# Half-precision pairs in the gating products, and a block of three experts in four column groups, in a kernel of mLSTM, spatial gating and sticky experts

## The chip, the cores and the metric

The kernel runs on one core of one Trainium2 chip. A core has a matrix engine (TensorE, in the profile PE; its weight loads are listed apart as PEld), three engines that work element by element (VectorE or DVE, ScalarE or ACT, GpSimdE or POOL), and SyncE (SP), which here only starts transfers between the chip's main memory and the core's memories. A matrix product on TensorE takes two operands: one of up to 128 columns is loaded into the array and stays ("weights"), the other streams through it column by column; the sums are written to PSUM, from which DVE or ACT must take them. The metric is the device time of one execution in microseconds (us); less is better.

## What is computed

Three layers follow one another, for 2 batches of 768 tokens (320 features in 8 heads of 40):

```python
# 1. mLSTM: a running matrix memory with gates (here worked out in chunks of 128 tokens)
C = f_stab * C + i_stab * outer(v, k); n = f_stab * n + i_stab * k
y = sigmoid(o_gate) * (C @ q) / max(|n . q|, 1)
# 2. gating products
h = relu(x @ w_in)                        # 320 -> 1024; u, v = the two halves
v_n = (v - mean) / sqrt(var + 1e-6)
v_s = w_spatial @ v_n + b_spatial         # mixes tokens
x2 = (u * v_s) @ w_out                    # 512 -> 320
# 3. eight experts; a token keeps the expert before it while sigmoid(x2 @ w_local) >= 0.5
e = argmax(x2 @ w_gate) or the token's predecessor's e
out = softmax(x2 @ w_gate)[e] * (relu(x2 @ w1[e]) @ w2[e])   # 320 -> 1024 -> 320
```

## The kernel before

**Exact products.** The choice of an expert hangs on small differences, so products are made of pairs: an operand is split into a high part and the remainder (low), and high x high, low x high and high x low are added up in PSUM. In layer 3 and in the token mixing the parts are F16 (`split`, `ws_piece`). In the gating products (x @ w_in and x2, with the tiles `wi`, `xh`, `xl`, `wo_h`, `wo_l`, `gt`) they are F32R, a rounded F32 format of four bytes that TensorE takes in one pass.

**Work of layers 1 and 2.** A chunk of 128 tokens is a number `i` from 0 to 11; `hf` from 0 to 3 is a group of three chunks, `dc` a block of 128 features. `do_ph(i)` makes the v half of x @ w_in, 8 matmuls of 512 columns for each of 12 chunks; `u_steps(hf, dc)` makes the u half, 8 matmuls of 384 columns for each of 16 pairs; `mix_steps` mixes tokens (18 F16 matmuls of 384 columns and one F32R) and multiplies by u; `x2_mm` makes x2, 12 matmuls for each of 12 chunks, of 330 columns in the first nine (10 for the expert choice) and 320 in the last three; `logits` makes the choice for the last three apart, 12 matmuls of 384 columns. `do_xh`/`do_xl`, `conv_in`, `conv_out`, `route_weights` and the end of `mix_steps` make the pairs, the high part on ACT and the remainder on DVE (some on POOL).

**Layer 3.** Tokens are sorted by expert into blocks of 128 rows: four early blocks (100 to 103) from batch 0 alone, five (0 to 4) of one expert each, three spare ones (6 to 8), and block 5, which three rarer experts share: `TILES = ((0, 32, 5), (32, 64, 6), (64, 128, 7))` gives rows 0 to 31 to expert 5, 32 to 63 to expert 6 and 64 to 127 to expert 7. A block is gathered (`gather`, POOL), turned (`turn_rows`), sent through w1 (`up_steps`: PSUM `phT`, then `hh` on ACT and `hl` on DVE, in two halves) and through w2 (`down`: 24 products, one for each of 8 row slices `fc` and 3 pairs, summed in PSUM `py`; then `yt` on ACT and a scatter on POOL). The weights come by SP into four staging tiles `stg` (`ld`) and are split on ACT and DVE (`sp`: `w2h`, then `w2l`). In block 5 each of the 24 products of `down` is three matmuls, one for each expert, whose loaded operand has 32, 32 and 64 columns; they write rows 0, 32 and 64 of `py`. Its result `yl` goes out last, behind a branch for further blocks (`last_blocks`) that this input doesn't take.

**What sets the order.** A table `ORDER` of 1,600 tokens (`bd.5` is the next piece of `down` for block 5) is written out by hand; each engine and each queue runs its own share strictly in that order, and waits on semaphores for the others.

Of the kernel before, what the change touches and what calls it, by code (L numbers as in the profile page):

```python
# [8 lines left out]
F32 = mybir.dt.float32  # L9
F32R = mybir.dt.float32r  # L10
# [33 lines left out]
S_K = 2.0 ** 4  # L44
X_TOP = 5
# [42 lines left out]
Lq.0 R.0 g.0 g.0 g.0 g.0 Lg.0 g.1 g.2 g.0 g.0 g.1 Lt.0 g.0 g.1 s0.0 Lv.0 g.0 g.0 g.1 C.0 s1.0 da.0 C.0 g.1 C.0 g.0 R.17  # L88
Lv.1 de.0 da.0 de.0 g.1 ds.0 C.0 R.1 co.0 g.1 Lq.1 ot.0 C.0 g.1 g.2 C.0 w0.0 g.2 Lt.1 C.1 w1.0 g.2 g.2 C.1 s2.0 w2.0
Lt.2 R.7 g.2 Lg.1 y0.0 g.1 k2.0 y1.0 y2.0 g.1 g.1 g.2 C.1 Lg.2 C.1 Lq.2 g.1 da.1 C.0 C.7 C.1 g.2 s2.1 g.2 g.2 da.1 U.0  # L90
ot.1 de.1 g.2 s0.1 de.1 R.2 g.2 da.2 dn.0 t1.0 xm.0 xc.0 px.0 um.0 Le.1 ds.1 co.1 Lv.2 g.2 w2.1 k2.1 de.2 da.3 C.0 C.1
Le.2 qg.1 da.2 s1.1 C.7 xh.0 U.1 C.2 w0.1 um.1 R.8 s0.2 de.2 xl.0 y0.1 ds.2 Lq.3 ot.2 C.2 co.2 C.1 C.2 Le.3 y2.1 w1.1
C.2 C.2 um.1 C.8 y1.1 C.1 s1.2 Lt.3 w1.2 ph.0 t1.1 Lg.3 ph.0 R.3 w0.2 de.3 k2.2 dn.1 C.8 s2.2 da.3 xm.1 qg.2 um.2 da.4
Lv.3 U.2 y0.2 C.2 C.2 xc.1 um.2 C.2 de.3 s0.3 w2.2 C.3 C.3 y1.2 y2.2 ph.0 s1.3 ds.3 Lg.4 co.3 C.3 qg.3 um.3 w0.3 t1.2
de.4 s2.3 C.3 C.3 px.1 C.3 dn.2 xh.1 da.4 y0.3 R.4 C.4 w2.3 rl.0 w1.3 xm.2 da.5 de.4 y2.3 Le.4 y1.3 xl.1 C.4 xc.2 da.5
Lg.5 ph.1 C.4 k2.3 C.4 U.3 dn.3 C.3 Lq.4 Lt.4 ds.4 co.4 R.5 C.4 bn.0 ot.3 s0.4 Lv.4 C.4 C.3 de.5 s2.4 t1.3 px.2 pw.0
Lq.5 xm.3 ph.1 w0.4 de.5 C.5 s1.4 um.3 Lt.5 w1.4 xh.2 qg.4 ds.5 ph.1 y0.4 xl.2 C.5 ph.2 Le.5 C.5 ot.4 w2.4 C.4 nw.0 ph.2
R.13 C.5 s1.5 C.4 xc.3 Lq.6 nw.0 k2.4 nh.0 y1.4 C.5 y2.4 s0.5 ph.2 C.5 rl.1 um.4 nl.0 Lv.5 w1.5 C.13 Lg.6 R.12 s2.5 C.5
dn.4 C.13 ds.6 qg.5 t1.4 U.4 Lv.6 rl.2 w2.5 um.4 R.14 u.0.0 w0.5 px.3 C.13 u.0.1 xh.3 C.5 de.6 bn.1 y0.5 ot.6 xm.4 C.13
# [62 lines left out]
def mlstm_sgu_sticky_moe(ctx: ExitStack, tc, qk, qk3, vko, ig, fg, w_in, w_out, w_sp, b_sp, w_gate, w_local, w1, w2, out):  # L162
# [132 lines left out]
    def f64_words(raw, n, out=None):  # L295
# [1254 lines left out]
```

## Time and profile before

| | |
|---|---|
| Median of 3 runs | 326.38 us (324.33 to 327.87) |
| Profiled execution, own time | 330.37 us |
| Its span, first to last instruction | 328.6 us |
| PE busy | 304.6 us (93%), 2685 matmuls |
| DVE busy | 263.1 us (80%) |
| ACT busy | 204.2 us (62%) |
| POOL busy | 108.8 us (33%) |
| DMA | 58.22 MB, 177 GB/s over the span |
| Mean granted TensorE clock | 0.996 of full |

The profiled execution is 3.99 us longer than the median of the runs. A matmul's end is modelled in the trace and reaches past the start of the next one, so "PE busy" says that something was under way, and what a matmul costs in a stream is read from the distance between starts.

### The profile page before, as it was taken

The page shows a single profiled execution, that of the slowest core. Times are in us where ns is not written, and L with a number is a line of the kernel's source. Part 1 is how long each engine was busy: PE and PEld are TensorE (multiplying, and loading weights), DVE is VectorE, ACT ScalarE, POOL GpSimd, SP SyncE. Part 2 cuts the span into 40 slices and gives each one's busy share as a digit, 9 for nine tenths or more (in the row PEclk, how much of TensorE's full clock was granted, in tenths as well). Part 3 has the DMA queues.
Part 4 walks back from the last instruction along what each step waited for, and adds up shares of the span by engine and source line. Part 5 has one row for each costly group of instructions (what it writes and reads, how often), then busy time and mean ns, then how long its engine had stood idle before and what let it go on. Part 6 is the DMA issues. An engine that isn't in the chain of part 4 may idle for free. (4 is left out here: it accounts for less than half of the span.)

```text
span 328.6 us, 7571 instructions
## 1 busy us (share of the span) xinstructions
PE 304.6 (93%) x2685; PEld 243.3 (74%) x2685; DVE 263.1 (80%) x655; ACT 204.2 (62%) x455; POOL 108.8 (33%) x150
## 2 busy tenths in 40 slices
PE   2499998999999999989999999999989999999991
PEld 1387895877885797669887677698968889888740
DVE  8999499998878988668776998799986957897810
ACT  1568387678697667683667665857466437666700
POOL 7585156342343202015421223600070605400401
PEclk9999999999999999999999999999999999999998
DMA  6857578665786474900016787796976765957500
GB/s 175 268 138 204 169 215 214 183 217 160 200 274 165 110 178 95 221 30 2 1 51 195 247 224 191 217 311 176 243 211 245 204 228 130 359 185 208 198 21 24
DMA packets 27707, 58.22 MB, mean 177 GB/s; under 512 B 5146, under 2 KB 15676, under 8 KB 27664
## 3 DMA queue, kind: packets, MB, share of 16 engines
q1 hardware_dynamic: 24258, 51.18, 53.7%
q0 software_dynamic: 1456, 4.53, 4.4%
q10 hardware_dynamic: 1950, 1.97, 2.3%
q8 instruction: 23, 0.38, 0.5%
q14 instruction: 20, 0.16, 0.2%
HBM read 53.25 MB, written 4.59 MB: 176 GB/s over the span
## 5 line engine op out<-in xcount | busy, mean ns | idle before, releaser
L1335 PE MATMUL phT<-xgT,w1all 128*128 128x128 f16 (+2 forms) x768 | 41.8, 210 | 0.0
L1335 PEld LDWEIGHTS <-w1all 128*128 128x128 f16 x768 | 39.1, 97 | 1.6
L577 PE MATMUL psS<-qbd,qk 120*128 120x384 f32 (+1 forms) x60 | 27.9, 561 | 10.4 <-DVE m L254 6.1
L790 PE MATMUL pv<-ws_h,vnh 128*128 128x384 f16 x96 | 31.3, 328 | 0.0
L790 PE MATMUL pv<-ws_h,vnl 128*128 128x384 f16 x96 | 31.3, 326 | 0.0
L790 PE MATMUL pv<-ws_l,vnh 128*128 128x384 f16 x96 | 31.3, 326 | 0.0
L1245 DVE SCALAR_TENSOR_TENSOR w2l<-stg,w2h 128x640 f16<-128x640 f32 x36 | 28.7, 819 | 3.1 <-ACT w2h L1243 3.0
L1356 PEld LDWEIGHTS <-hh 128*128 128x128 f16 (+2 forms) x240 | 22.0, 98 | 10.7
L1243 ACT ACTIVATE w1all<-stg 128x1024 f16<-128x1024 f32 (+1 forms) x24 | 22.2, 946 | 10.3 <-DMA stg<-in_moe_w_dram 3.9
L790 PEld LDWEIGHTS <-vnh 128*128 128x128 f16 x192 | 18.6, 97 | 13.5 <-issue 0.8
L1305 POOL DMA_INDIRECT xg<-rows_d,gidx x9 | 10.8, 1203 | 51.3 <-DVE w1all L1262 25.8
L1243 ACT ACTIVATE w2h<-stg 128x640 f16<-128x640 f32 x36 | 25.2, 730 | 3.2 <-DMA stg<-in_moe_w_dram 3.0
L492 POOL TENSOR_SCALAR_AFFINE_SELECT gbc<-gbc 128x512 f32<-128x512 f32 (+1 forms) x18 | 17.4, 967 | 28.8 <-DVE lg L843 10.8
L1245 DVE SCALAR_TENSOR_TENSOR w1all<-stg,w1all 128x1024 f16<-128x1024 f32 (+1 forms) x24 | 26.4, 1103 | 0.5 <-ACT w1all L1243 0.5
L837 PE MATMUL po<-wo_h,gt 128*128 128x330 f32 (+1 forms) x96 | 24.4, 328 | 1.2 <-DVE ut L796 1.2
L1356 PE MATMUL py<-w2h,hl 128*128 128x320 f16 (+2 forms) x88 | 23.7, 303 | 0.0
L1356 PE MATMUL py<-w2h,hh 128*128 128x320 f16 (+2 forms) x88 | 23.7, 303 | 0.0
L1356 PE MATMUL py<-w2l,hh 128*128 128x320 f16 (+2 forms) x88 | 23.7, 303 | 0.0
L1340 ACT ACTIVATE hh<-phT 128x512 f16<-128x512 f32 x26 | 15.3, 592 | 12.5 <-PE phT L1335 12.3
L724 PE MATMUL ph<-wi,xh 128*128 128x512 f32 x60 | 22.8, 457 | 0.0
L1342 DVE SCALAR_TENSOR_TENSOR hl<-phT,hh 128x512 f16<-128x512 f32 x26 | 17.8, 686 | 6.0 <-ACT hh L1340 5.7
L584 DVE TENSOR_TENSOR gbc<-psS,gbc 128x384 f32<-128x384 f32 (+1 forms) x36 | 17.6, 501 | 5.3 <-PE psS L577 5.1
(320 smaller groups left out, 833.8 us busy)
## 6 DMA issues: line engine op xcount, KB each, us to landing
stg<-in_moe_w_dram SPq DMA_DIRECT2D x22, 640.0 KB
stg<-in_moe_w_dram SPq DMA_DIRECT2D x16, 512.0 KB
vko<-in_vko_dram SPq DMA_DIRECT2D x12, 504.5 KB
gbc<-scg SPq DMA_DIRECT2D x6, 512.0 KB
qk<-in_qk_dram SPq DMA_DIRECT2D x8, 360.0 KB
ws<-in_moe_w_spatial_dram SPq DMA_DIRECT2D x6, 384.0 KB
raw<-in_moe_w_in_dram SPq DMA_DIRECT2D x4, 512.0 KB
stg<-in_moe_w_dram SPq DMA_DIRECT2D x8, 256.0 KB
```

The source lines that it names most:

```text
L492: nc.gpsimd.affine_select(out=dm, in_=dm, pattern=[[0, n], [1, P]], compare_op=ALU.is_ge, fill=fill, base=0, channel_multiplier=-1)
L577: nc.tensor.matmul(ps[:, :n * P].rearrange("p (a s) -> p a s", a=n), u["kT"][:, g, :], u["qbd"][:, g:g + 3 * n - 2:3], start=True, stop=True)
L584: nc.vector.tensor_tensor(w, u["ps", g][:, :n * P].rearrange("p (a s) -> p a s", a=n), w, ALU.mult)
L724: nc.tensor.matmul(u["ph"], x_[:, sl], wi[:, wk, DH:], start=(n == 0), stop=(n == len(terms) - 1))
L790: nc.tensor.matmul(pv, x_[i][:, ds_], w_[:, c, ts_], start=False, stop=(n == 18))
L837: nc.tensor.matmul(pos[i], gx[hf, dc][:, sl], wx[:, dc, :cols], start=(n == 0), stop=(n == 11))
L1243: nc.scalar.activation(hi, src, AF.Copy, scale=scale)
L1245: nc.vector.scalar_tensor_tensor(lo, src, scale, hi, ALU.mult, ALU.subtract)
L1335: nc.tensor.matmul(ph[:, f * P + t0:f * P + t1], w_[fc // 2][:, wk, (fc % 2) * P:(fc % 2 + 1) * P], xT[:, xk, t0:t1], start=(n == 0), stop ...
L1340: nc.scalar.activation(hh[:, hs], pf, AF.Relu)
L1342: nc.vector.scalar_tensor_tensor(hl[:, hs], pf, 0.0, hh[:, hs], ALU.max, ALU.subtract)
L1356: nc.tensor.matmul(py[t0:t1], h_[:, fc, t0:t1], ws[w_][:, fc], start=(n == 0), stop=(n == 23))
```

## The change

Layer 2 gets four new scales, powers of two, so that scaling rounds nothing. The tiles `wi`, `wo_h`, `wo_l`, `xh`, `xl` and `gt` become F16. Copies on ACT become copies with a scale, subtractions on DVE become scale-and-subtract, and where sums leave PSUM the scale is taken out again in an instruction that was there before. In `down`, block 5's expert 7 gets two matmuls of 32 loaded columns in place of one of 64. `ORDER` is a new table of the same 1,600 tokens. The copy of the index column `sidx` in the branch stands in both kernels.

```diff
+S_X = 2.0 ** 9
+S_WI = 2.0 ** 6
+S_G = 2.0 ** 10
+S_WO = 2.0 ** 6
 ORDER = '''
-Lq.0 R.0 g.0 g.0 g.0 g.0 Lg.0 g.1 g.2 g.0 g.0 g.1 Lt.0 g.0 g.1 s0.0 Lv.0 g.0 g.0 g.1 C.0 s1.0 da.0 C.0 g.1 C.0 g.0 R.17
+Lg.0 Lv.0 g.0 g.0 g.1 Lq.0 Lt.0 R.0 Lg.1 R.1 g.0 g.0 g.0 s0.0 ot.0 g.0 s2.0 g.0 g.1 g.0 g.2 g.1 g.1 C.0 C.0 g.1 C.0 g.0
...
-    wi = l2.tile([P, 5, DF], F32R, name="wi")
-    wo_h = lk.tile([P, 4, 330], F32R, name="wo_h")
-    wo_l = lk.tile([P, 4, 330], F32R, name="wo_l")
+    wi = l2.tile([P, 5, DF], F16, name="wi")
+    wo_h = lk.tile([P, 4, 330], F16, name="wo_h")
+    wo_l = lk.tile([P, 4, 330], F16, name="wo_l")
...
-            nc.scalar.copy(wi[:, kc, cs], t)
+            nc.scalar.activation(wi[:, kc, cs], t, AF.Copy, scale=S_WI)
             yield
-            nc.vector.tensor_tensor(wi[:, 2 + kc, cs], t, wi[:, kc, cs].bitcast(F32), ALU.subtract)
+            nc.vector.scalar_tensor_tensor(wi[:, 2 + kc, cs], t, S_WI, wi[:, kc, cs], ALU.mult, ALU.subtract)
...
-            xh[hf] = l2.tile([P, 3, HALF], F32R, tag="xh", name="xh", bufs=2)
-            xl[hf] = l2.tile([P, 3, HALF], F32R, tag="xl", name="xl", bufs=2)
+            xh[hf] = l2.tile([P, 3, HALF], F16, tag="xh", name="xh", bufs=2)
+            xl[hf] = l2.tile([P, 3, HALF], F16, tag="xl", name="xl", bufs=2)
...
-        nc.vector.tensor_tensor(xl[hf][:, :, sl], st[i]["px"].rearrange("p (k s) -> p k s", k=3),
-                                xh[hf][:, :, sl].bitcast(F32), ALU.subtract)
+        nc.vector.scalar_tensor_tensor(xl[hf][:, :, sl], st[i]["px"].rearrange("p (k s) -> p k s", k=3), S_X,
+                                       xh[hf][:, :, sl], ALU.mult, ALU.subtract)
...
-        gt = lk.tile([P, 2, HALF], F32R, tag="g", name="gt", bufs=8)
+        gt = lk.tile([P, 2, HALF], F16, tag="g", name="gt", bufs=8)
...
-            parts = [(t0, t1, w2t[e]) for t0, t1, e in TILES]
+            parts = [(t, t + 32, w2t[e]) for t0, t1, e in TILES for t in range(t0, t1, 32)]
```

The first place at which instructions move is TensorE in `down` of block 5, the last work of TensorE (`py_5253` before and `py_5250` after; the third number is how many columns of the operand are loaded, then how many stream). Before:

```order
L1356 LDWEIGHTS hh_4977
L1356 MATMUL py_5253<-w2h_2972,hh_4977 32x320
L1356 LDWEIGHTS hh_4977
L1356 MATMUL py_5253<-w2h_5095,hh_4977 32x320
L1356 LDWEIGHTS hh_4977
L1356 MATMUL py_5253<-w2h_5133,hh_4977 64x320
```

After:

```order
L1361 LDWEIGHTS hh_4966
L1361 MATMUL py_5250<-w2h_3054,hh_4966 32x320
L1361 LDWEIGHTS hh_4966
L1361 MATMUL py_5250<-w2h_4995,hh_4966 32x320
L1361 LDWEIGHTS hh_4966
L1361 MATMUL py_5250<-w2h_5169,hh_4966 32x320
L1361 LDWEIGHTS hh_4966
L1361 MATMUL py_5250<-w2h_5169,hh_4966 32x320
```

Of each of the 24 products, the matmul with 64 loaded columns has become two with 32.

The second place is DVE just before the branch, at the same point of the program: the remainders of the last weights (`w2l`) and of the second half of block 5 (`hl`, the row whose PSUM tile is `phT_5138` before and `phT_5142` after). Before:

```order
L1245 SCALAR_TENSOR_TENSOR w2l_5134<-stg_5101,w2h_5133 128x640
L1245 SCALAR_TENSOR_TENSOR w2l_5096<-stg_4870,w2h_5095 128x640
L1245 SCALAR_TENSOR_TENSOR w2l_5134<-stg_5101,w2h_5133 128x640
L1342 SCALAR_TENSOR_TENSOR hl_4978<-phT_5138,hh_4977 128x512
L1245 SCALAR_TENSOR_TENSOR w2l_5134<-stg_5239,w2h_5133 128x640 x2
```

After:

```order
L1250 SCALAR_TENSOR_TENSOR w2l_5170<-stg_4936,w2h_5169 128x640
L1250 SCALAR_TENSOR_TENSOR w2l_5170<-stg_5108,w2h_5169 128x640
L1250 SCALAR_TENSOR_TENSOR w2l_5170<-stg_4936,w2h_5169 128x640
L1347 SCALAR_TENSOR_TENSOR hl_4967<-phT_5142,hh_4966 128x512
L1250 SCALAR_TENSOR_TENSOR w2l_5170<-stg_5108,w2h_5169 128x640
```

One remainder of the last weights now stands behind `hl`, where two stood.

The third place is the start of x2 on TensorE. Before, an F32R matmul loads its own operand within one instruction:

```order
L837 MATMUL po<-wo_h,gt 128x330 x2
L837 MATMUL po<-wo_l,gt 128x330
L837 MATMUL po<-wo_h,gt 128x330 x2
L837 MATMUL po<-wo_l,gt 128x330
L837 MATMUL po<-wo_h,gt 128x330 x4
```

After, each F16 matmul has a load of its own in front of it:

```order
L842 LDWEIGHTS gt
L842 MATMUL po<-wo_h,gt 128x330
L842 LDWEIGHTS gt
L842 MATMUL po<-wo_h,gt 128x330
L842 LDWEIGHTS gt
L842 MATMUL po<-wo_l,gt 128x330
```

Number and sizes of the matmuls of layer 2 are as before.

## Rows read from the trace of the kernel before

**Rows 1.** Busy time by stage: stretch, its length, busy us of each engine (instructions), clock, DMA share, GB/s.

```profile
6.00:40.00 34.00, 29.32 (x113) 22.26 (x114) 28.59 (x63) 19.16 (x55) 18.87 (x16) 1.00 0.67 199
40.00:140.00 100.00, 96.66 (x650) 77.64 (x649) 86.76 (x229) 73.79 (x197) 32.18 (x32) 1.00 0.69 187
140.00:172.00 32.00, 30.60 (x224) 26.78 (x223) 25.25 (x88) 20.75 (x53) 11.56 (x47) 1.00 0.06 21
172.00:220.00 48.00, 47.58 (x360) 34.96 (x359) 41.09 (x125) 31.30 (x61) 14.28 (x12) 1.00 0.76 227
220.00:310.00 90.00, 88.45 (x1281) 76.77 (x1278) 74.12 (x138) 54.82 (x87) 24.71 (x20) 1.00 0.74 223
310.00:328.60 18.60, 11.99 (x75) 4.85 (x72) 2.69 (x4) 2.79 (x5) 1.96 (x2) 0.93 0.07 21
```

**Rows 2.** Instructions in order of time, end of the program: start, length (us), engine, line.

```profile
303.08 0.33 SPq L1270 DMA_DIRECT2D stg<-in_moe_w_dram  x1
...
310.55 0.59 ACT L1340 ACTIVATE hh<-phT 128x512 f16<-128x512 f32 x1
...
311.02 1.36 ACT L1243 ACTIVATE w2h<-stg 128x640 f16<-128x640 f32 x2
311.17 0.69 DVE L1342 SCALAR_TENSOR_TENSOR hl<-phT,hh 128x512 f16<-128x512 f32 x1 [0.67 <-ACT hh L1340]
...
311.79 1.56 DVE L1245 SCALAR_TENSOR_TENSOR w2l<-stg,w2h 128x640 f16<-128x640 f32 x2
...
322.02 0.53 ACT L1364 ACTIVATE yl<-py,xg 128x320 f32<-128x320 f32 x1 [9.64 <-PE py L1356]
322.83 0.98 POOL L1372 DMA_INDIRECT out_dram<-yl,sidx  x1 [10.92 <-ACT yl L1364]
```

**Rows 3.** Block 5's `down` on PE, in order of time: first product, second, last.

```profile
310.00 0.31 PE L1356 MATMUL py<-w2h,hh 128*32 128x320 f16 x2
...
310.24 0.32 PE L1356 MATMUL py<-w2h,hh 128*64 128x320 f16 x1
310.49 0.31 PE L1356 MATMUL py<-w2h,hl 128*32 128x320 f16 x2
...
321.42 0.57 PE L1356 MATMUL py<-w2l,hh 128*32 128x320 f16 x3
```

**Rows 4.** Streams of F16 matmuls on PE, 320 columns (seven), then 384 (seventeen).

```profile
292.30 0.30 PE L1356 MATMUL py<-w2h,hh 128*128 128x320 f16 x1
...
293.12 0.30 PE L1356 MATMUL py<-w2h,hh 128*128 128x320 f16 x1
...
203.49 0.33 PE L790 MATMUL pv<-ws_h,vnl 128*128 128x384 f16 x1
...
206.09 0.33 PE L790 MATMUL pv<-ws_l,vnh 128*128 128x384 f16 x1
```

**Rows 5.** Streams of F32R matmuls on PE: 512 columns, 384 (from first to last eight), 330 (twelve).

```profile
145.58 0.86 PE L724 MATMUL ph<-wi,xh 128*128 128x512 f32 x3
146.28 0.39 PE L724 MATMUL ph<-wi,xl 128*128 128x512 f32 x1
...
152.12 0.68 PE L771 MATMUL pu<-xh,wi 128*128 128x384 f32 x3
...
153.36 0.34 PE L771 MATMUL pu<-xl,wi 128*128 128x384 f32 x1
...
158.22 0.46 PE L837 MATMUL po<-wo_h,gt 128*128 128x330 f32 x2
...
159.88 0.31 PE L837 MATMUL po<-wo_l,gt 128*128 128x330 f32 x1
```

**Rows 6.** Groups of DVE and ACT instructions: shapes, count, busy us, mean ns, idle before.

```profile
L765 DVE TENSOR_TENSOR vnl<-vr,vnh 128x512 f16<-128x512 f32 x5 | 3.4, 683 | 0.8 <-ACT vnh L762 0.8
L599 DVE SCALAR_TENSOR_TENSOR wl<-gbc,wh 128x512 f16<-128x512 f32 x4 | 2.7, 681 | 0.0
...
L776 ACT ACTIVATE ut<-pu 128x384 f32<-128x384 f32 x12 | 5.8, 480 | 1.9 <-PE pu L771 1.9
L703 ACT CAST xh<-px 128x384 fp32r<-128x384 f32 x12 | 5.7, 476 | 1.5 <-PE px L695 1.3
```

**Rows 7.** Waits of PE over the whole span: total us, times, longest.

```profile
PE psS L577 <- DVE m L254: 6.1, 1, 6.1
PE psS L577 <- DVE gbc L584: 4.3, 2, 3.8
```

More of the change, by code (lines that the diff above doesn't have):

```diff
@@ L158 @@
+bp.7 bu.7 bd.6 bd.6 bu.8 sp.44 sp.44 bu.8 bu.7 sp.44 bu.7 sp.42 sp.42 bd.4 bu.8 bu.7 bu.8 sp.42 bd.6 tr.5 ld.33 sp.43
+bu.7 bu.8 bu.7 ld.34 bd.7 bu.8 bd.7 bu.7 bd.7 tr.5 sp.44 ld.38 sp.45 bd.7 bu.8 bd.3 bu.5 sp.45 sp.45 sp.33 bu.8 sp.33
+sp.34 bu.5 bu.8 bu.5 sp.45 bu.5 bu.8 sp.34 bu.5 bd.8 bu.8 bu.8 ld.39 sp.34 bd.8 sp.33 bd.8 bu.5 bd.8 bd.7 bu.5 sp.33
+sp.34 sp.38 sp.39 sp.38 bd.7 sp.39 bu.5 bu.5 bu.5 bd.5 sp.38 bd.8 sp.38 bd.6 bu.5 bd.8 sp.39 bu.5 bd.5 sp.39 bd.5 bd.5
+bd.5 bd.5
 '''
@@ L336, in conv_in @@
         if kc < 2:
-            nc.scalar.copy(wi[:, kc, cs], t)
+            nc.scalar.activation(wi[:, kc, cs], t, AF.Copy, scale=S_WI)
             yield
-            nc.vector.tensor_tensor(wi[:, 2 + kc, cs], t, wi[:, kc, cs].bitcast(F32), ALU.subtract)
+            nc.vector.scalar_tensor_tensor(wi[:, 2 + kc, cs], t, S_WI, wi[:, kc, cs], ALU.mult, ALU.subtract)
         else:
-            nc.scalar.copy(wi[:, 4, cs], t)
+            nc.scalar.activation(wi[:, 4, cs], t, AF.Copy, scale=S_WI)
             yield
-            nc.vector.tensor_tensor(wi[64:, 4, cs], t[64:], wi[64:, 4, cs].bitcast(F32), ALU.subtract)
+            nc.vector.scalar_tensor_tensor(wi[64:, 4, cs], t[64:], S_WI, wi[64:, 4, cs], ALU.mult, ALU.subtract)
         yield
@@ L355, in conv_out @@
             yield
-        nc.scalar.copy(wo_h[:, kc, :DM], t)
+        nc.scalar.activation(wo_h[:, kc, :DM], t, AF.Copy, scale=S_WO)
         yield
-        nc.vector.tensor_tensor(wo_l[:, kc, :DM], t, wo_h[:, kc, :DM].bitcast(F32), ALU.subtract)
+        nc.vector.scalar_tensor_tensor(wo_l[:, kc, :DM], t, S_WO, wo_h[:, kc, :DM], ALU.mult, ALU.subtract)
         yield
@@ L390, in route_weights @@
             yield
-            nc.scalar.copy(wo_h[:, dc, DM:330], ps)
+            nc.scalar.activation(wo_h[:, dc, DM:330], ps, AF.Copy, scale=S_WO)
             yield
-            nc.vector.tensor_tensor(wo_l[:, dc, DM:330], ps, wo_h[:, dc, DM:330].bitcast(F32), ALU.subtract)
+            nc.vector.scalar_tensor_tensor(wo_l[:, dc, DM:330], ps, S_WO, wo_h[:, dc, DM:330], ALU.mult, ALU.subtract)
             yield
@@ L801, in mix_steps @@
         yield
-        (nc.vector if hf < 2 or (hf, dc) in GLV else nc.gpsimd).tensor_tensor(gl[hf, dc], g32, gh[hf, dc].bitcast(F32), ALU.subtract)
+        (nc.vector if hf < 2 or (hf, dc) in GLV else nc.gpsimd).tensor_tensor(gl[hf, dc], g32, gh[hf, dc], ALU.subtract)
     lg = const.tile([P, NT, 10], F32, name="lg")
@@ L842, in x2_scale_steps @@
         if i < 9:
[L843 removed]
+            nc.vector.tensor_scalar(lg[:, i, :], po[:, DM:330], 1.0 / (S_G * S_WO), None, ALU.mult)
             yield
```

145 lines of the change are left out of this document (70 added, 75 removed).

## The prediction

> **What bounds the kernel now.** I read the busy time by stage first. The reader is to see that TensorE (PE) is busy 96.66 of 100 us from 40 to 140, 30.60 of 32 up to 172, 47.58 of 48 up to 220 and 88.45 of 90 up to 310, while DVE, the next, has 86.76, 25.25, 41.09 and 74.12 [rows 1]. From 40 us on PE is the bound, with DVE close behind it in the first of these stages. In the 34 us before, PE has 29.32, and its two longest kinds of waits there are for DVE, 6.1 us (of which the start of the program is a part) and 4.3 us [rows 7]. The row that stands out is the last: after 310 us PE is busy 11.99 us with only 75 matmuls, and DVE and ACT have 2.69 and 2.79 us between them and the end [rows 1].
>
> So I read the end next, in order of time. The last transfer of weights starts at 303.08. After 310 ACT and DVE finish the second half of block 5 (`hh`, then `hl`) and two last pieces of weights (`w2h`, then `w2l`, done at 313.35), and then nothing but PE works; ACT waits 9.64 us until `yl` at 322.02, and POOL 10.92 us until the scatter at 322.83 [rows 2]. What PE does there is `down` of block 5: its first product starts at 310.00, its 24th at 321.42, that is 11.42/23 = 0.497 us for each. Within a product the two matmuls of 32 loaded columns start together at 310.00 (x2, 0.31 us long, as one of them is), the one of 64 columns at 310.24, and the next product at 310.49 [rows 3]. So two run side by side, then a third follows 0.24 us later, and the next pair 0.25 us after that. A matmul of 320 columns in a stream with the whole array takes (293.12 - 292.30)/6 = 0.137 us [rows 4]: more than 0.1 us is lost at each change between 32 and 64 columns, and the third matmul doesn't share the array with the other two.
>
> **Block 5 in groups of 32 columns.** Before, from the first start to `yl`: 322.02 - 310.00 = 12.02 us, 0.36 of it from the last matmul's start (321.42 + 0.24) to `yl` [rows 2, 3]. After, each product is four matmuls of one size on four parts of the array. No row has four of them, so I bound a product's step: below by 0.137, the stream itself; above by 0.25, the distance that follows the single 64 column matmul, if what is lost there comes with each new set of loaded operands and not with the change of size [rows 3, 4]. I take 0.14, since the row nearest to it is the pair that starts together: side by side is what these groups do. Then 23 x 0.14 + 0.36 = 3.6 us, a gain of **8.4 us**; at 0.25 it is 6.1 us, a gain of 5.9.
>
> The Trainium skill bears on which of the two it is. "TensorEngine Tiling (Array Packing)", section Key Properties, says that tiles work independently and that changing the tiling mode, not just the tile, drains the engine; by that the loss belongs to the change of size, no product of the new kernel pays it, and the gain is 12.02 - (23 x 0.137 + 0.36) = 8.5 us. The same page, Gotcha 2, speaks against the change: column tiling excludes the fast weight load, so that four slow loads would stand in each product; if they showed, the step would go towards 0.25.
>
> The cover must hold: products 13 to 24 need `hl`, the last six the last `w2l`. Counted from the end of block 5's up products, and with the lengths of before, `hh` is done after some 0.7 us (0.59 and the start), `hl` after 1.4 (0.69), the one `w2l` that the new order leaves behind it after 2.2 (1.56/2) [rows 2]. Product 13 comes at 12 x 0.14 = 1.7, product 19 at 2.5. Both are in time by 0.3 us; with both `w2l` still behind `hl`, as before, the end would have been some 0.5 late. If the last transfer came later against PE than now (7 us before PE's last stage [rows 2]), this cover would be the first to go.
>
> **F16 for F32R.** An F32R matmul of 512 columns takes 0.70/3 = 0.233 us in a stream, of 384 columns 1.24/7 = 0.177, of 330 columns 1.66/11 = 0.151 [rows 5]. F16 takes 0.137 for 320 and 2.60/16 = 0.1625 for 384 [rows 4], 0.0004 us a column; I estimate 0.141 for 330 and 0.214 for 512 by that line. By the counts of the code: `do_ph` 96 x 0.019 = 1.8; `u_steps` 128 x 0.0145 = 1.9; `x2_mm` 144 x 0.010 = 1.4 (the 36 of 320 columns taken alike); `logits` 12 x 0.0145 = 0.2. In all 5.3 us of PE, spread over 40 to 220 us. The separate loads of F16 are in these steps already, since the F16 streams of rows 4 have a load for each matmul. At most all of it shortens the run, PE being 96 to 99% busy there; at least nothing, if DVE, at 87% in the longest stage with as many instructions as before, holds the order back [rows 1]. I take two thirds, **3.5 us**, because PE is nearer to full than DVE, but each of its waits for DVE stays as long as it is.
>
> **The rest.** Scale-and-subtract takes 681 ns where a subtraction of the same size takes 683, and a scaled copy to F32 480 ns where a copy to F32R takes 476 [rows 6]: 0 for the pairs, within 0.2 us either way for some 40 of them, which lie under PE. The new order runs the same 1,600 tokens. I can read from it where instructions stand, not what they wait; I take 0, and for the range a gain or a loss of up to 4.3 us, the size of PE's second longest kind of wait [rows 7].
>
> **Sum.** 8.4 + 3.5 = 11.9 us. The profiled execution takes 330.37 us (a span of 328.6 and 1.8 around it), so it would take 318.5. It is 3.99 us longer than the median of the runs, and the terms are lengths of PE's own work, the same in both; from the median, 326.38 - 11.9 = **314.5 us**.
>
> **Rivals.** *Each set of operands pays the loss.* A product of block 5 takes 0.25 us, and 326.38 - 5.9 - 3.5 = 317.0. For it: every step between sets in the row is 0.24 or 0.25 and none 0.137 [rows 3]. Against it: every such step is also a change of size. 1 in 10.
>
> *DVE or ACT take back the F16 part.* The products of layer 2 end sooner and PE waits for `xl`, `gt` or attention's results instead: 326.38 - 8.4 = 318.0. For it: DVE's 86.76 of 100 us [rows 1]. Against it: nearly all of PE's waits there are short. 17 in 100.
>
> *The four groups take turns (slower).* If matmuls of one expert's operands and another's don't overlap but each pays 0.25, a product takes 1.0 us and `down` 23 x 1.0 + 0.75 + 0.36 = 24.1 us in place of 12.0: 326.38 + 12.1 - 3.5 = 335.0. It decides from the point where a product takes over 0.497 + 3.5/23 = 0.65 us. Against it stands the pair at 310.00 [rows 3]. 3 in 100.
>
> *The new order costs waits of its own.* A PE wait of 4.3 us, the size of one that stands there now [rows 7], gives 318.8, and two of them 323.1, no change. 7 in 100, at 319 to 326.
>
> *The new order is better too.* All of the F16 part and 4.3 us of waits at the start: 326.38 - 8.4 - 5.3 - 4.3 = 308.4. 5 in 100.
>
> **How the numbers follow.** That leaves 58 in 100 for the forecast, 314.5, itself between 311.5 and 317 (the F16 part between 0.9 and its whole, the order by about 1 us). The range from 310 to 320.5 holds it, the first two rivals and a third of the fourth, about 86 in 100; a tighter one would drop a rival that the rows can't settle. One percent is 3.3 us, about what a measurement can tell from no change (the three runs lie 3.5 apart). Under 323.1 lie the forecast, the first two rivals, the last and most of the fourth less a little for what I haven't thought of: 0.90 faster; 0.06 the same; 0.04 slower, from turns and a bad order.
>
> **What would show it.** Right: four matmuls of block 5 start together, products 0.14 us apart, `yl` some 3.6 us after the first; `ph` in F16 in steps of 0.21 to 0.22; DVE's groups as long as before; PE's waits in the first 40 us within 4 us of before. Wrong: steps of 0.25 in block 5; PE waiting in its middle for `w2l` or `hl`; PE's busy share falling below 95% between 40 and 220 us, with DVE named as releaser; or the end of block 5's up products not 2 to 5 us earlier than 310.

## The result, and the profile after

| | before | after |
|---|---|---|
| Median of 4 runs each, one chip | 327.12 us (324.33 to 328.84) | 317.62 us (316.33 to 317.73) |
| Ratio, with its 95% interval | 1 | 0.9709 (0.9633 to 0.9784) |
| Profiled execution, own time | 330.37 us | 317.73 us |
| Its span | 328.6 us | 316.0 us |
| PE busy | 304.6 us, 2685 matmuls | 289.1 us, 2709 matmuls |
| DVE busy | 263.1 us | 260.6 us |

The change takes 9.5 us off the median, 2.9%; 11.9 were forecast. A second comparison (`e10_after`, below) gave 7.7 us, 0.9739 (0.9689 to 0.9789). The two profiled executions lie 12.6 us apart, more than either: that of before was one in which the start ran late, which is explained below. Ratios leave out single executions that ran over 1.5% longer than the fastest of their kernel, so a ratio can say a little more or less than the medians beside it.

Busy time by stage after (columns as in [rows 1]):

```profile
6.00:40.00 34.00, 27.10 (x111) 21.03 (x112) 27.94 (x61) 19.12 (x55) 16.02 (x17) 1.00 0.63 184
40.00:140.00 100.00, 98.33 (x675) 69.51 (x674) 89.49 (x237) 78.47 (x207) 33.96 (x71) 1.00 0.69 189
140.00:172.00 32.00, 32.00 (x260) 20.86 (x258) 26.91 (x111) 21.81 (x50) 8.19 (x9) 1.00 0.24 78
172.00:220.00 48.00, 47.30 (x424) 32.51 (x422) 42.95 (x120) 32.52 (x63) 13.63 (x11) 1.00 0.77 224
220.00:310.00 90.00, 84.36 (x1248) 72.06 (x1244) 68.73 (x118) 50.59 (x80) 23.74 (x21) 0.98 0.67 206
```

From 40 to 172 us PE is fuller than in [rows 1] and puts more matmuls through the same time (935 in place of 874). The last row already holds block 5 whole, and 5.6 of its 90 us are without work, of which only 1.7 come after the last matmul.

Instructions in order of time at the end of the program, the answer to [rows 2, 3]:

```profile
304.85 0.32 PE L1361 MATMUL py<-w2h,hh 128*32 128x320 f16 x4
...
304.99 0.31 PE L1361 MATMUL py<-w2h,hl 128*32 128x320 f16 x4
...
305.58 0.69 DVE L1347 SCALAR_TENSOR_TENSOR hl<-phT,hh 128x512 f16<-128x512 f32 x1 [0.18 <-ACT hh L1345]
...
306.21 0.83 DVE L1250 SCALAR_TENSOR_TENSOR w2l<-stg,w2h 128x640 f16<-128x640 f32 x1
...
307.98 0.31 PE L1361 MATMUL py<-w2l,hh 128*32 128x320 f16 x4
308.37 0.53 ACT L1369 ACTIVATE yl<-py,xg 128x320 f32<-128x320 f32 x1 [2.19 <-PE py L1361]
310.34 0.98 POOL L1377 DMA_INDIRECT out_dram<-yl,sidx  x1 [4.09 <-DVEq L1497]
```

The four matmuls of a product start together (x4), the next product follows after 0.14 us, the 24th starts (307.98 - 304.85) = 3.13 us after the first, 0.136 each, and `yl` 3.52 us after it, in place of 12.02. What is new stands in the last row. `yl` ends at 308.90, but the scatter starts only at 310.34, 1.44 us later, released by DVE's queue at L1497, the branch; in [rows 2] it came 0.28 us after `yl` ended.

Streams of F16 matmuls of the gating products, the answer to [rows 5]:

```profile
148.23 0.44 PE L842 MATMUL po<-wo_h,gt 128*128 128x330 f16 x2
...
149.35 0.30 PE L842 MATMUL po<-wo_l,gt 128*128 128x330 f16 x1
...
154.88 0.65 PE L776 MATMUL pu<-xh,wi 128*128 128x384 f16 x3
155.37 0.33 PE L776 MATMUL pu<-xl,wi 128*128 128x384 f16 x1
...
155.86 0.59 PE L729 MATMUL ph<-wi,xh 128*128 128x512 f16 x2
156.29 0.38 PE L729 MATMUL ph<-wi,xl 128*128 128x512 f16 x1
```

330 columns take (149.35 - 148.23)/8 = 0.140 us from start to start, 384 take 0.163, 512 take 0.215, where F32R took 0.151, 0.177 and 0.233 [rows 5]. The elementwise groups that answer to [rows 6] cost nearly the same as before, 482 ns for 480 and 488 for 476 (and `xl`, the scale-and-subtract on DVE, 546 for 542):

```profile
L781 ACT ACTIVATE ut<-pu 128x384 f32<-128x384 f32 x12 | 5.8, 482 | 1.1 <-PE pu L776 1.0
L708 ACT ACTIVATE xh<-px 128x384 f16<-128x384 f32 x12 | 5.8, 488 | 1.5 <-PE px L700 1.5
```

Waits of PE over the span, the answer to [rows 7]:

```profile
PE psS L582 <- DVE gp L280: 8.0, 1, 8.0
PE psS L582 <- DVE gbc L589: 3.7, 1, 3.7
...
PE py L1361 <- DVE hl L1347: 1.9, 1, 1.9
```

The first matmul comes 1.9 us later than before (8.0 for 6.1), and the last row is a wait that before doesn't have. Its place, in order of time:

```profile
259.95 1.06 ACT L1248 ACTIVATE w1all<-stg 128x1024 f16<-128x1024 f32 x1 [0.97 <-DVE w1t L1387]
260.92 0.51 ACT L1369 ACTIVATE yt<-py,xg 128x320 f32<-128x320 f32 x1
261.33 1.07 ACT L1345 ACTIVATE hh<-phT 128x512 f16<-128x512 f32 x2
...
262.46 0.31 PE L1361 MATMUL py<-w2h,hh 128*128 128x320 f16 x1 [0.76 <-ACT hh L1345]
262.67 1.22 DVE L1267 SCALAR_TENSOR_TENSOR w1all<-stg,w1all 64x1024 f16<-64x1024 f32 x1
...
263.92 0.69 DVE L1347 SCALAR_TENSOR_TENSOR hl<-phT,hh 128x512 f16<-128x512 f32 x1
...
264.67 0.45 PE L1361 MATMUL py<-w2h,hl 128*128 128x320 f16 x1 [1.90 <-DVE hl L1347]
...
265.18 0.47 PE L1361 MATMUL py<-w2h,hh 128*128 128x320 f16 x1
```

On ACT, `hh` of blocks 3 and 2 stands behind a piece of weights that itself waits until DVE has copied `w1t`; on DVE, `hl` stands behind another piece of weights. PE waits 0.76 and 1.90 us. And its matmuls of 320 columns then start 0.27 us apart, not 0.136: from 264 to 268 us the granted clock was 0.57, near the lower level, 1.2 GHz:

```profile
264.00:268.00 4.00, 3.33 (x13) 1.89 (x14) 2.83 (x6) 0.45 (x1) 0.79 (x1) 0.57 0.48 134
```

### The profile page after: what moved, and what is told of

It is laid out like the page before. It is cut to its first block, busy times and chain, and to the rows that moved or that the text cites. A ratio compares the mean times of both kernels' runs of the same rounds, so it can differ in the third digit from the quotient of the medians.

```text
span 316.0 us, 7616 instructions
## 1 busy us (share of the span) xinstructions
PE 289.1 (91%) x2709; PEld 216.0 (68%) x2709; DVE 260.6 (82%) x655; ACT 204.1 (65%) x455; POOL 101.7 (32%) x150
## 5 line engine op out<-in xcount | busy, mean ns | idle before, releaser
L582 PE MATMUL psS<-qbd,qk 120*128 120x384 f32 (+1 forms) x60 | 26.4, 549 | 11.7 <-DVE gp L280 8.0
L1361 PEld LDWEIGHTS <-hh 128*128 128x128 f16 (+1 forms) x256 | 20.9, 99 | 8.3 <-ACT hh L1345 0.9
L497 POOL TENSOR_SCALAR_AFFINE_SELECT gbc<-gbc 128x512 f32<-128x512 f32 (+1 forms) x18 | 16.0, 895 | 31.9 <-ACT gbc L536 16.3
L1361 PE MATMUL py<-w2h,hl 128*128 128x320 f16 (+1 forms) x96 | 22.3, 306 | 1.9 <-DVE hl L1347 1.9
L582 PEld LDWEIGHTS psS<-qbd,qk 120*128 120x128 f32 x60 | 12.1, 226 | 16.2 <-DVE gp L280 7.9
L1361 PE MATMUL py<-w2h,hh 128*128 128x320 f16 (+1 forms) x96 | 22.3, 307 | 0.8 <-ACT hh L1345 0.8
L1361 PE MATMUL py<-w2l,hh 128*128 128x320 f16 (+1 forms) x96 | 22.3, 306 | 0.0
L842 PE MATMUL po<-wo_h,gt 128*128 128x330 f16 (+1 forms) x96 | 21.7, 302 | 0.0
L1310 POOL DMA_INDIRECT xg<-rows_d,gidx x9 | 9.8, 1091 | 36.4 <-ACT yt L1369 32.3
L661 PEld LDWEIGHTS Y<-vko,gbc 128*128 128x128 f32 x128 | 19.8, 227 | 1.4 <-issue 0.9
```

The lines of the kernel that those rows point to most:

```text
L497: nc.gpsimd.affine_select(out=dm, in_=dm, pattern=[[0, n], [1, P]], compare_op=ALU.is_ge, fill=fill, base=0, channel_multiplier=-1)
L582: nc.tensor.matmul(ps[:, :n * P].rearrange("p (a s) -> p a s", a=n), u["kT"][:, g, :], u["qbd"][:, g:g + 3 * n - 2:3], start=True, stop=True)
L661: nc.tensor.matmul(yh, u["dm"][:, h], u["v"][:, h], start=(C is None), stop=last)
L842: nc.tensor.matmul(pos[i], gx[hf, dc][:, sl], wx[:, dc, :cols], start=(n == 0), stop=(n == 11))
L1310: nc.gpsimd.indirect_dma_start(out=xgs[blk], out_offset=None, in_=src, in_offset=bass.IndirectOffsetOnAxis(ap=ix, axis=0))
L1361: nc.tensor.matmul(py[t0:t1], h_[:, fc, t0:t1], ws[w_][:, fc], start=(n == 0), stop=(n == 23))
```

## The experiments

**Theory** after reading the two traces: block 5 gains its 8.5 us and gives some 1.1 back at the branch; F16 gains what was forecast; the new order costs some 3 us net, at the start and near 262 us. **Rivals**: F16 gains nothing since DVE holds the order back; or the order costs nothing and its stalls stand in place of others. Three sets of four kernels ran, each set on one chip beside runs of the kernel before: medians of before are 324.14 us in the first set, 333.02 in the second, 324.36 in the third. Ratios are to before of the same set.

### Each part alone: e1_groups, e2_order, e3_f16, e4_f16_order

`e1_groups` is the kernel before with this line alone:

```diff
-            parts = [(t0, t1, w2t[e]) for t0, t1, e in TILES]
+            parts = [(t, t + 32, w2t[e]) for t0, t1, e in TILES for t in range(t0, t1, 32)]
```

> The kernel before with block 5's `down` in four groups of 32 alone: F32R pairs and the order of before stay. Theory (products 0.136 us apart, and of the 8.4 us won about 1.1 given back, since the last scatter now waits for DVE behind the branch): some 7.3 us less than before, ratio about 0.978, with the step of a product near 0.14 us and the scatter more than 1 us after `yl`. With the order of before two pieces of `w2l` stand behind `hl`, so a wait of up to 0.5 us may show between the 18th and 19th product. Rival, no loss at the branch: 8.4 us less, 0.974. Rival, each set of operands pays: 5.9 us less, 0.982, steps of 0.25.

Measured: 318.24 us, 5.9 less, 0.9815 (0.9729 to 0.9902). The interval holds the theory's 0.978 and both rivals (0.974 and 0.982) too, so the time doesn't tell them apart; the trace does. Its end in order of time:

```profile
304.65 0.31 PE L1356 MATMUL py<-w2h,hh 128*32 128x320 f16 x4
...
305.79 0.32 PE L1356 MATMUL py<-w2h,hl 128*32 128x320 f16 x4 [0.83 <-issue]
...
308.77 0.53 ACT L1364 ACTIVATE yl<-py,xg 128x320 f32<-128x320 f32 x1 [2.58 <-PE py L1356]
310.41 0.98 POOL L1372 DMA_INDIRECT out_dram<-yl,sidx  x1 [4.81 <-ACTq L1492]
```

Products are 0.14 us apart here too, not 0.25. A gap of 1.0 us came between the fourth and the fifth product, not in the middle as expected, and the trace names nothing for it ("issue"); it didn't come in the changed kernel. The scatter again stands 1.1 us behind the end of `yl` (309.30), so something is given back at the branch here too. This trace puts it down to ACT's queue at the branch, not to DVE's; `e6_no_copy` below tests which.

`e2_order` is the kernel before with the new table alone (its first lines stand in the diff above).

> The kernel before with the new order alone: F32R pairs and block 5 with its 64 columns stay. Theory (the new order brings the stall that the changed kernel shows at 260 to 268 us, 2.7 us of waits and 1.6 us at the lower clock): 2 to 4.5 us more than before, ratio 1.006 to 1.014, with PE waiting for `hl` in that place. Rival, the order is neutral, the stall standing in place of smaller ones of before: within 1 us, 1.000. Rival, the order is better elsewhere: 2 to 4 us less, 0.988 to 0.994.

Measured: 329.19 us, 5.1 more, 1.0199 (1.0133 to 1.0265). The theory's direction, and a little more than its range; both waits, 0.8 for `hh` and 1.9 for `hl`, are in its trace.

`e3_f16` is the changed kernel with the table and the `parts` line of before; `e4_f16_order` has that line of before alone:

```diff
-            parts = [(t, t + 32, w2t[e]) for t0, t1, e in TILES for t in range(t0, t1, 32)]
+            parts = [(t0, t1, w2t[e]) for t0, t1, e in TILES]
```

> The kernel before with F16 pairs alone: the order of before and block 5 with its 64 columns stay. Theory of the prediction (two thirds of the 5.3 us that PE's matmuls lose): 3.5 us less than before, ratio 0.989, PE's share from 40 to 140 us near 97% as before. Rival, DVE or ACT hold the order back: 0 to 1 us less, 0.997 to 1.000, PE's share in that stretch some points lower. Rival, all of it: 5.3 us less, 0.984.

Measured: 322.35 us, 1.8 less, 0.993 (0.9891 to 0.9968), between theory and rival; the interval just shuts out both.

> The changed kernel with block 5's `down` put back to 32, 32 and 64 columns: F16 pairs and the new order. Theory: the time of the changed kernel and the 7.3 us that the groups bring net of the branch, so 2 us less than before, ratio 0.993, with no wait behind the branch. Rival, nothing lost at the branch: 1 us less, 0.997. If F16 pays its 3.5 us and the order costs nothing, 0.989.

Measured: 325.61 us, 1.5 more than before, 1.0052 (1.001 to 1.0095), outside all three. Against `e2_order` it shows F16 under the new order: 329.19 - 325.61 = 3.6 us. Under the order of before F16 gave 1.8. By the intervals above, the two aren't clearly apart. One row of each trace speaks for a real difference (busy time from 40 to 180 us; the first number behind the length is PE), for `e1_groups`, `e3_f16`, `e2_order` and `e4_f16_order` in turn:

```profile
40.00:180.00 140.00, 135.97 (x920) 109.44 (x919) 119.12 (x344) 100.82 (x255) 45.83 (x82) 1.00 0.55 153
```

```profile
40.00:180.00 140.00, 132.15 (x925) 88.81 (x925) 119.01 (x345) 101.38 (x254) 44.52 (x81) 1.00 0.55 153
```

```profile
40.00:180.00 140.00, 138.98 (x956) 113.50 (x956) 120.00 (x361) 103.84 (x263) 43.78 (x81) 1.00 0.57 160
```

```profile
40.00:180.00 140.00, 138.20 (x978) 94.86 (x977) 123.14 (x368) 105.17 (x267) 45.15 (x82) 1.00 0.59 163
```

With the order of before, F16 takes PE's share from 135.97 to 132.15: much of what the shorter matmuls save turns into waiting, at unchanged DVE. The waits that grew are mostly those for ACT, from 0.2 to 2.7 us; those for DVE go from 3.7 to 4.2. With the new order PE stays at 138 to 139 us and does 22 matmuls more. In this stage the new order is the better one, and F16 pays more under it. The order must lose elsewhere, then.

### What a product pays for: e13_sizes_apart

The kernel before with `down` of block 5 in two passes:

```diff
-                for (t0, t1, ws) in parts:
+                for (t0, t1, ws) in parts[:2]:
...
+        n = 0
+        for fc in range(8):
+            for (h_, w_) in ((hh, 0), (hl, 0), (hh, 1)):
+                for (t0, t1, ws) in parts[2:]:
```

> The kernel before with block 5's products in another order: first all 48 matmuls of 32 loaded columns, then all 24 of 64, so that one change of size is left in place of 47. Theory (the loss of more than 0.1 us comes with each change of size): both rows in steps of 0.136 to 0.14, `down` of block 5 takes 48 x 0.137 = 6.6 us in place of 12.0, and the run 5 us less than before, ratio 0.984. Rival (each new set of operands pays): steps of 0.24 to 0.25, 12 us, no change, 1.000.

Measured: 320.19 us, 4.2 less by the medians; by the ratio, 0.9839 (0.9774 to 0.9904), 5.2, near the 5 of the theory. PE in order of time:

```profile
308.32 0.31 PE L1356 MATMUL py<-w2h,hh 128*32 128x320 f16 x2
308.46 0.30 PE L1356 MATMUL py<-w2h,hl 128*32 128x320 f16 x2
...
312.07 0.30 PE L1356 MATMUL py<-w2l,hh 128*32 128x320 f16 x2
312.31 0.32 PE L1364 MATMUL py<-w2h,hh 128*64 128x320 f16 x1
312.47 0.30 PE L1364 MATMUL py<-w2h,hl 128*64 128x320 f16 x1
```

Pairs of 32 columns follow each other 0.14 us apart, those of 64 after the first step as well (23 steps in 3.15 us, 0.137 each), and the only step of 0.24 us is the one from 32 to 64. One other step is longer: at the 14th pair PE waits for `hl`, which stands apart from this question. Each set of operands is new, and only the change of size costs. That settles the prediction's first rival.

### The order of before under the other two parts: e5_f16_groups

The changed kernel with the table of before.

> The changed kernel with the order of before: F16 pairs and four groups of 32 stay. Theory (the new order costs more than it gives: the start runs at half pace until 39 us and not until about 31, and 4.5 us are lost at 260 to 268 us): less than the changed kernel by 2 to 5 us, that is a ratio to before of 0.958 to 0.968, with no wait of PE over 1 us between 240 and 300 us and a wait of some 0.8 us for `w2l` or `hl` in block 5. Rival, the new order is what makes the groups pay and the changed kernel is the better: 0.972 to 0.98.

Measured: 324.99 us, 0.975 (0.9697 to 0.9804). The rival's number: two kernels with the new order, each with one more small edit that is told below, took 319.69 and 320.11 us in the same set. So my reading that the whole order of before was better fell. On this chip two stalls stood in layer 3 under the order of before that its other traces don't have. Instructions in order of time:

```profile
257.46 1.08 ACT L1344 ACTIVATE hh<-phT 128x512 f16<-128x512 f32 x2 [3.27 <-remote]
...
303.56 0.26 PE L1339 MATMUL phT<-xgT,w1all 128*128 128x32 f16 x4 [0.48 <-issue]
```

ACT stood still for 3.27 us before `hh`, and PE got its short matmuls of 32 columns in bunches. The trace names no engine as releaser in either place, and what they waited for stays open.

### Three losses of the changed kernel, each alone and together: e6, e7, e9 to e12

`e6_no_copy` takes out the only instruction that ties the last scatter to DVE in the branch:

```diff
         last_blocks(NS + N_SURE, NBLK)
-        nc.vector.tensor_copy(sidx[:, NS - 1:NS], sidx[:, NS - 1:NS])
     scatter(NS - 1, box["yl"])
```

> The changed kernel without the index copy on DVE in the branch, the one thing in it that ties the last scatter to DVE's way past the branch; the branch isn't taken, so the output is the same. Theory (the scatter waits for DVE's branch): the scatter comes 0.3 us after `yl` ends, as before, in place of 1.44, and the run takes 1.1 us less than the changed kernel, 0.3%, ratio to before 0.967. Rival (POOL's own way past the branch is as late as DVE's): the scatter stays 1.4 us behind `yl`, no change.

Measured: 319.69 us, 0.9591 (0.9516 to 0.9666), in the set where before took 333.02. In order of time:

```profile
312.74 0.53 ACT L1369 ACTIVATE yl<-py,xg 128x320 f32<-128x320 f32 x1 [1.91 <-PE py L1361]
313.54 0.98 POOL L1377 DMA_INDIRECT out_dram<-yl,sidx  x1 [4.24 <-ACT yl L1369]
```

The scatter comes 0.27 us after `yl` ends (313.27), released by ACT: the wait for DVE's way past the branch is shown. In the seven traces that keep the copy and whose `yl` comes early (the changed kernel twice, `e1_groups`, `e5_f16_groups`, `e7_mended`, `e9_warm`, `e11_start`), the scatter starts 3.22 to 3.53 us after DVE's last work. What the wait is worth in the run isn't shown, since the changed kernel didn't run in this set, and 1.16 us (1.44 - 0.28) is less than the interval.

`e7_mended` exchanges twelve neighbours in the table:

```diff
-bu.2 bd.102 bp.6 ld.30 sp.31 bd.1 bu.3 bu.2 bu.3 bd.2 sp.32 bu.2
+bu.2 bd.102 bd.2 bu.3 bu.2 bp.6 bu.3 bu.2 ld.30 sp.31 bd.1 sp.32
```

> The changed kernel with twelve neighbours of the order exchanged near 260 us: both halves' `hh` come ahead of a piece of weights on ACT, both `hl` ahead of one on DVE. Theory (the order of ACT and DVE there makes PE wait 2.7 us, and then its matmuls take 0.27 us in place of 0.136 for 3 us): neither wait nor slow matmuls show between 255 and 270 us, and the run takes 3 to 4.5 us less than the changed kernel, ratio to before 0.957 to 0.962. Rival (the wait only moves to the next piece of weights): within 1 us of the changed kernel, 0.968 to 0.974, with a PE wait of 1 us or more before 285.

Measured: 314.45 us, 0.9433 (0.9379 to 0.9486), 5.2 less than `e6_no_copy` and 5.7 less than `e9_warm` in the same set. The place in order of time:

```profile
260.05 1.05 ACT L1342 ACTIVATE hh<-phT 128x512 f16<-128x512 f32 x2
...
260.99 1.28 DVE L1344 SCALAR_TENSOR_TENSOR hl<-phT,hh 128x512 f16<-128x512 f32 x2
...
262.24 0.30 PE L1358 MATMUL py<-w2h,hh 128*128 128x320 f16 x1
262.38 0.30 PE L1358 MATMUL py<-w2h,hl 128*128 128x320 f16 x1
```

`hh` is done before PE comes, both `hl` just when it does; PE doesn't wait, and starts its matmuls 0.136 us apart. Neither wait came back elsewhere: behind 60 us PE has none of over 0.8 us. By the rows of the changed kernel the stall cost 4.3 us: 2.7 of waits, and 1.6 in which 12 matmuls took 0.13 us more each at the lower clock. The lower clock doesn't always follow: of the seven profiles that have this place as the new order left it, six show a granted clock of 0.57 to 0.70 over 4 us there, but `e2_order`, with the same two waits, keeps 1.00, and its matmuls start 0.14 us apart right behind the wait:

```profile
269.67 0.31 PE L1357 MATMUL py<-w2h,hl 128*128 128x320 f16 x1 [1.90 <-DVE hl L1343]
269.81 0.30 PE L1357 MATMUL py<-w2l,hh 128*128 128x320 f16 x1
```

The start. The same two matmuls of `psS` (384 columns) take, in the profiled execution of before and in `e1_groups`, whose program is the same up to there:

```profile
35.53 1.63 PE L577 MATMUL psS<-qbd,qk 120*128 120x384 f32 x2
```

```profile
33.69 0.89 PE L577 MATMUL psS<-qbd,qk 120*128 120x384 f32 x2
```

By the lengths of its matmuls PE runs at half its later pace until some moment: 31.7 us in `e1_groups`, 39.1 in the execution of before. Of the seven profiled executions that begin in the order of before, four change over at 30 to 32 us (`e1_groups`, `e3_f16`, `e5_f16_groups`, `e12_all`) and three at 39 to 40 (before, `e11_start`, `e13_sizes_apart`); those three took 4 to 6 us more than the medians of their kernels. The seven that begin in the new order all change at 39 to 42 us. The granted clock doesn't tell the two apart. From 30 to 39 us, `e1_groups` and the changed kernel both have 1.00 (2.4 GHz), but 59 matmuls in one and 42 in the other:

```profile
30.00:39.00 9.00, 9.00 (x59) 7.46 (x59) 6.66 (x17) 5.38 (x17) 4.18 (x4) 1.00 0.65 208
```

```profile
30.00:39.00 9.00, 9.00 (x42) 7.78 (x41) 5.12 (x16) 4.91 (x15) 3.78 (x6) 1.00 0.58 177
```

`e9_warm` fills PE's first waits with matmuls nobody reads:

```diff
+    def keep_busy(k):
+        ps = bank("YU", "idle")
+        for n in range((11, 7, 2)[k]):
+            nc.tensor.matmul(ps.rearrange("p (a s) -> p a s", a=4), ones_b, ones_b.unsqueeze(1).broadcast_to((P, 4, P)), start=True, stop=True)
...
```

Three entries in the table place the calls.

> The changed kernel with 20 matmuls of constants, whose results nobody reads, where PE waits in the first 25 us: 11 ahead of its first product, 7 in the wait at 11.6 to 15.3 us, 2 ahead of the wait at 24.1 us. Theory (PE's matmuls take twice their later time until it has been busy without longer gaps, in the changed kernel until 39.1 us, and the new order's gaps at the start are what it pays): the step from half to full pace comes before 32 us, matmuls of `psS` (384 columns) between 20 and 39 us take half as long, and the run takes 3 to 5 us less, ratio to before 0.955 to 0.962. Rival (the start is bound by DVE and by loads, pace or not): 0 to 1 us less, 0.968 to 0.971.

Measured: 320.11 us, 0.961 (0.9543 to 0.9678), no better than `e6_no_copy` beside it. The theory fell: full pace came at 40.0 us, and now the granted clock did show it, 0.50 (1.2 GHz) over the stretch in which the kernels above have 1.00:

```profile
30.00:39.00 9.00, 9.00 (x41) 7.72 (x41) 5.12 (x15) 4.89 (x16) 3.79 (x6) 0.50 0.58 188
```

More work for PE there didn't bring the pace forward.

The last set ran the changed kernel again, and beside it `e11_start`, the changed kernel with the first 171 of the 1,600 steps in the order of before, and `e12_all`, which has that start, the exchange of `e7_mended` and the missing copy of `e6_no_copy`.

> The changed kernel as it is, so that the next two stand beside it on one chip: ratio to before 0.963 to 0.978, as in its first comparison. Expected of its trace, by the theory that its losses are the order's own: half pace until about 39 us, the waits of 0.8 and 1.9 us near 262 to 265 us with slow matmuls behind them, and the scatter 1.4 us or more behind `yl`.

Measured: 316.65 us, 0.9739 (0.9689 to 0.9789), with all three losses in its trace.

> The changed kernel with the first 171 steps of its order (some 40 us) taken from the order of before, the others following in the new order. Theory (the new order's start keeps PE at half pace until 39 us or later, that of before until 31 or 32): full pace from about 31 us, and 3 to 4 us less than the changed kernel on the same chip, 1.0%. Rival (the place of the step to full pace is chance, since the profiled run of before had it at 39 us too): within 1 us of the changed kernel. Rival (the spliced order brings waits at its seam): the step at 31 us, and still no gain.

Measured: 312.42 us, 0.9603 (0.9537 to 0.9669), 4.2 less than the changed kernel. Its profiled execution was one in which the pace rose late (39.5 us), and at 318.26 us the slowest of its four, as slow as the changed kernel (315.95 to 318.58 in this set); the other three took 310.8 to 313.5. So the gain seems to go with the early rise, and to come partly by chance: in these runs the order of before makes the early rise possible, not certain.

> The changed kernel with the start of the order of before, the twelve neighbours near 260 us exchanged, and without the index copy in the branch; the branch isn't taken, so the output is the same. Theory (three losses, each apart from the others): 3.5 for the start, 4.5 for the waits near 262 us, 1.1 for the branch, 9 us less than the changed kernel on the same chip, ratio between the two 0.971. Rival (they overlap, or the mended place only hands its wait on): 4 to 5 us less, 0.985.

Measured: 307.5 us, 0.9447 (0.9366 to 0.9528): 9.15 us less than the changed kernel where 9 were expected, and 16.9 less than before. In its profile full pace comes at 30.2 us, PE waits nowhere for `hh` or `hl`, block 5 starts at 296.02, and the scatter follows the end of `yl` by 0.47 us. It is the fastest kernel of this study.

## Why the prediction came out as it did

**Block 5: right.** Step 0.136 for the 0.14 taken, 3.52 us for 3.6, a gain of 8.5 for 8.4. The cover held as worked out: counted from the end of the up products (304.85), `hh` was done after 0.70 us (0.7), `hl` after 1.42 (1.4), the `w2l` after 2.19 (2.2), and no product waited. The rule on changes of the tiling mode that the prediction cited from the Trainium skill ("TensorEngine Tiling (Array Packing)", Key Properties) agrees with `e13_sizes_apart`: 0.24 us at the one change of size, 0.14 in the stream on either side. The slow loads that the prediction took from its Gotcha 2 didn't show in a step.

**What follows block 5: missed.** The sum ended at `yl`. Behind it the scatter waits for DVE as well, which signals from behind the branch some 3 us after its last work (307.04, scatter 310.34). Before, DVE was through long ago, since `yl` came 9 us after it was done [rows 2]. So 1.16 us of the 8.5 (1.44 - 0.28) were given back to a wait that had always been there, under cover. Naming what stands behind the last instruction that gets faster would have found it: the code has the copy in the branch.

**F16: right in size, for a reason that the prediction didn't have.** The estimates of 0.214 and 0.141 us came out as 0.215 and 0.140. Of the 5.3 us of PE's work 3.6 became time under the new order, as forecast (3.5), but 1.8 under that of before, halfway to the rival that DVE or ACT take it back. Under that order the waits that grew were mostly those for ACT. So the two thirds came out under the one order and not under the other; what share pays seems to be a matter of the order, though the two gains aren't clearly apart by their intervals.

**The new order: the step that failed.** It was put at 0, with 4.3 us either way for the range. (The rivals call 4.3 us the size of one wait; [rows 7] give it as two waits, the longest 3.8.) Alone it costs 5.1 us (`e2_order`), with F16 3.3 (`e4_f16_order` against `e3_f16`), both in the first set; in the second set kernels with it were some 5 us faster than `e5_f16_groups`, so its sign isn't the same in all sets. By the traces this is a sum of large terms of both signs: it fills some 6 us of PE's idle time between 40 and 180 us (with F16, 138.20 of 140 us busy in place of 132.15), and loses some 4 at the start (`e11_start`) and 4.3 near 262 us (2.7 in the profile of `e2_order`, where the clock stayed up). The rival "costs waits of its own", 7 in 100, at 318.8 us for one wait of 4.3, describes the outcome best: the 317.62 us lie outside the forecast's own range (311.5 to 317) and inside the whole one. One of the prediction's signs of being wrong was met by a little: block 5's `down` starts at 304.85, 5.15 us before 310.00, where 2 to 5 were allowed. Both profiles have a late start, so the loss at the start doesn't enter that difference.

**The base.** The prediction noted that the profiled execution was 3.99 us above the median, and took the terms to be the same in both. They are, but the rows didn't show what a usual execution of before does at its start: in that profile PE changed pace at 39.1 us, as in every profile of a kernel that starts in the new order, and so the loss at the start couldn't be seen by comparing the two profiles. That its usual executions change earlier is inferred, from the other kernels that start in the order of before and from the 4 us by which this execution lies above the median; no such execution of before itself was profiled. Among profiles with a late start the order even looks like a gain: spans of 328.6 us for before and 326.7 for `e2_order`, then 323.5 with F16 and 316.0 with the groups.

**The sum.** By the parts, -8.5 + 1.2 - 3.6 + 5.1 = -5.8 us; two comparisons gave 7.7 and 9.5. The part of block 5 holds: `e4_f16_order` and the changed kernel, which differ in it alone, start block 5 at 304.92 and 304.85, and their spans are 323.5 and 316.0 us, 7.5 apart for 7.3 of the sum. So by these profiles the remaining 2 to 4 us lie in the order and F16 against before, and aren't settled: the ten runs of `e4_f16_order` alone lie 5.4 us apart, and chips differ in what the order is worth (the set of `e5_f16_groups` speaks for the new order by 5 us). That the forecast came within 2.4 us of the measured gain is in part luck, then: it had the order at nothing, and what the order costs or gives changed from set to set.

## What to carry over

When the last instructions get faster, ask what stands behind them and what else it waits for: a branch or a wait that cost nothing under a long product becomes the end once that product is short. A rewritten order isn't a zero term: go through it stage by stage, ask at each place where weights and results share an engine whether the result that TensorE needs stands first, and test splices of old and new order, since parts of each can be better. Before trusting one profile as the base, look at what in it differs from the median run.

## What was unexpected about the chip

- Matmuls of one size on four column groups run fully side by side, 0.136 us for four of 320 columns, as long as for one; a change between 32 and 64 loaded columns costs 0.10 to 0.11 us more.
- What waits for DVE behind a branch that isn't taken starts some 3 us after DVE's last work (3.30 in the changed kernel, 307.04 to 310.34; 3.26 in `e1_groups`, where DVE ended at 307.15; 3.22 to 3.53 in seven traces). What takes this time isn't shown.
- After waits of 0.76 and 1.90 us the granted clock was 0.57 over the next 4 us, so that 2.7 us of waits cost 4.3. In `e2_order` it stayed at 1.00 after the same waits; what decides is open.
- At the start PE runs at half its later pace until 30 to 42 us, in some stretches with a granted clock of 1.00 in the record. Twenty idle matmuls didn't end it sooner. What decides when it ends is open.
- The kernel before took 324 to 327 us in three sets of runs and 333 in the one in which kernels with the new order took 319 to 320; why the order of before does less well on that chip wasn't found out.
